# Last tile of a two-layer Fourier and expert kernel: scores read from PSUM, whole blocks exchanged over two queues, put-off rows added by accumulating transfers

## The chip, the cores and the metric

The kernel runs on one core of one Trainium2 chip. The metric is the device time of one execution in microseconds (us), the median of several runs. The engines of a core work from instruction queues of their own, in order, and wait for each other through semaphores: TensorE (PE in the profile, its weight loads PEld) multiplies matrices into PSUM, VectorE (DVE) and ScalarE (ACT) work on the on-chip memories SBUF and PSUM, GpSimd (POOL) on SBUF, and SyncE (SP) issues most transfers. The transfers of all queues run on 16 DMA engines.

## The reference

Two layers work on x, 2048 tokens of 512 numbers. Each layer adds a Fourier mixing of the normalised rows, and then a sum over experts picked by product keys:

```python
x = x + _A_ref(_layernorm(x), dft_seq_re, dft_seq_im, dft_hid_re, dft_hid_im)
x = x + _B_ref(_layernorm(x), w_q, k1, k2, u, v)      # and both once more

# _A_ref: the real part of a two-dimensional Fourier transform, by matrices
y = einsum("ts,bse->bte", seq_re, x @ hid_re.T) - einsum("ts,bse->bte", seq_im, x @ hid_im.T)

# _B_ref: 32 heads, 2 x 16 keys each, 2 x 2 best, of these the 2 best of 256 experts
s1, s2 = q1 @ k1.T, q2 @ k2.T                          # per token and head, 16 scores each
t1, i1 = the two largest of s1;  t2, i2 = the two largest of s2
cand = t1[:, None] + t2[None, :];  eidx = i1[:, None] * 16 + i2[None, :]
g, e = softmax of the two largest of cand, their eidx
out = sum over heads and picks of g * gelu(x . u[e]) * v[e]
```

## The kernel before

**Tiles.** The 2048 tokens are 16 tiles of 128 (`P`). The sequence transform of a layer is done in units: seven of two tiles (256 tokens) and two of one tile (tiles 14 and 15). In layer 1 the units run in the order 0, 7, 1 to 6, 8, so tiles 12 and 13 (unit 6) come last but one and tile 15 (unit 8) last. `seq_unit` multiplies the normalised rows (`xh`, `xl`, high and low parts) with the sequence matrices (`ch`, `cl`) into `acc` (L519); `token_tile` does the rest for one tile.

**One tile** (`token_tile`). TensorE multiplies the transform with the hidden matrices (L659), VectorE adds it to the row (L669), statistics are taken (L255 to L264, one step on GpSimd, L261), the row is scaled (L272, L697), transposed (L747 or through memory) and cast in two parts (L752, L757). TensorE makes 2 x 512 scores into two PSUM banks `pc` (L777, L781), ScalarE copies them to `sc` in SBUF, reordered (L786). VectorE picks the best two of 16 keys for each of 64 half-heads: a tree of maxima (L867, L876, the helper `tree32`), a comparison with the maximum (`eq`, L861), its number (L903, L885), the removal of that entry (L912, L916), and the same again. From the picks (`q`) TensorE turns codes (L989), ScalarE copies them (`qt`, L993), VectorE makes one-hot masks (L1012, L1018), TensorE multiplies these in blocks of four tokens (L1028), and ScalarE copies the blocks to SBUF (L1038): a block is 4 x 4 small matrices of which the diagonal is wanted. That diagonal goes out to memory in four transfers and comes back, one token per partition, in two (`gdr`, `gt`; L1058, L1066). VectorE multiplies it with the activation (L1069), TensorE transposes it (L1100) and multiplies it with the expert values `vh`, `vl` in six steps (L1119, L1123). VectorE adds the product to the row (L1134), and SyncE stores the row (L1139).

**Put-off products.** For the 13 tiles of the first seven units of layer 1 that last product is put off (`DEFERRED`): the weights go to memory (`ptd`, L1091), the row to `xod`, and `off(z, ...)` does the rest in the last stretch, as soon as TensorE is done with the sequence transform: load the weights (L574), cast (L581), load the row (L585), six products into `acc` (L591), a copy by ScalarE (L597), a sum by VectorE (L600), a store (L601).

**Order.** Nothing is written out in its final order. Each step is an `Op` with its engine, a cost and a priority; `Plan.run` places them on the engines by these costs, and the program is emitted in that order. Each engine then runs its own list in order. Tile 15 has the priority `FINAL` and the flag `fine`: its first sum and scaling are done in halves, and its selection (`HALVED`) in two halves whose steps alternate. Where the plan sees a gap on TensorE after the last sequence product, it puts filler products in (L1205).

```python
a = op("PE", MM512, f, a0 + [a, seq_last], take=[hb] if n == 0 else [], prio=prio + (n,))
nc.scalar.copy(t["sc"][:, :, hf, :], t["pc", hf].rearrange("p h e -> p e h"))
nc.sync.dma_start(t["gdr"][:, :, k].rearrange("j e g f -> (j e) g f"), t["gs"][k::4, :, k, :])
```

## Time and profile before

| what | us |
|---|---|
| median of 3 runs | 1251.66 |
| lowest and highest | 1251.53, 1252.41 |
| the profiled execution, whole | 1250.42 |
| its span, first to last instruction | 1248.7 |
| TensorE busy | 1226.5 (98%) |
| VectorE busy | 1009.6 (81%) |
| ScalarE busy | 483.2 (39%) |
| granted TensorE clock | 1.000 |

The profile is of one execution; its times run from the start of the span. A busy time is the sum of an engine's instructions; neighbours on VectorE and TensorE overlap a little, so the distance from start to start is what a queue pays. A row of the order of time gives start, duration, engine, line and operation with `out<-in`, and how many were merged.

### The profile page before, as it was taken

The numbers are of one execution on the slowest core, as the hardware profiler recorded it, in microseconds if no ns is written. First come the engines' busy times: TensorE is split into PE (matmuls) and PEld (weight loads), VectorE is DVE, ScalarE is ACT, GpSimd is POOL, SyncE is SP. The second block draws the span as 40 slices with busy tenths as digits, with TensorE's granted clock in tenths as the row PEclk, the third lists the DMA queues.
The fourth block names the chain that finished last, engine by engine and source line by source line (L and its number), as shares of the span: only waits on it lengthen the run. The fifth ranks groups of instructions, "written<-read, shape, count | busy, mean of one in ns | idle before, by whom it ended". The sixth has DMA issues, their size and how long they took to land.

```text
span 1248.7 us, 20707 instructions
## 1 busy us (share of the span) xinstructions
PE 1226.5 (98%) x7576; PEld 1015.0 (81%) x7576; DVE 1009.6 (81%) x2290; ACT 483.2 (39%) x994; POOL 44.5 (4%) x71
## 2 busy tenths in 40 slices
PE   9999999999999999999999999999999999999997
PEld 6877778777887888899878888777888888888985
DVE  8899997988988876869877458969595877969797
ACT  7522244333333333433563233333333333333543
POOL 2000000000000000000000000000000000000000
PEclk9999999999999999999999999999999999999999
DMA  7866551343434244341556232443526343353554
GB/s 239 263 197 223 179 159 35 85 89 93 99 92 105 67 100 111 76 119 58 129 135 153 93 104 54 122 101 90 139 76 144 85 110 85 102 118 94 127 169 127
DMA packets 317766, 148.19 MB, mean 119 GB/s; under 512 B 221920, under 2 KB 287968, under 8 KB 317664
## 3 DMA queue, kind: packets, MB, share of 16 engines
q1 hardware_dynamic: 317664, 146.87, 44.3%
q8 instruction: 59, 0.97, 0.3%
q14 instruction: 43, 0.35, 0.1%
HBM read 120.86 MB, written 25.95 MB: 118 GB/s over the span
## 4 chain that ended last, share of the span: by engine, by line
PE 64%; DVE 20%; issue 6%; DMA 5%; ACT 2%; SPq 2%; POOL 1%; POOLq 0%; DVEq 0%; ACTq 0%
PE acc L519 36%; PE bank L659 9%; PE bank L777 6%; PE bank L781 3%; DVE cl L463 2%; PE bank L808 2%; DVE eq L861 2%; DVE w L385 1%; DMA raw<-x2d 1%; PE bank L519 1%; DVE lr L1012 1%; PE bank L393 1%; DVE tmp L867 1%; DVE eq L885 1%; DMA gdr<-sc 1%
## 5 line engine op out<-in xcount | busy, mean ns | idle before, releaser
L519 PE MATMUL acc<-ch,xh 128*128 128x512 f32 (+1 forms) x868 | 328.7, 379 | 1.7 <-DVE ptl L548 1.7
L519 PE MATMUL acc<-cl,xh 128*128 128x512 f32 (+1 forms) x868 | 321.9, 371 | 0.0
L519 PE MATMUL acc<-ch,xl 128*128 128x512 f32 (+1 forms) x868 | 321.8, 371 | 0.0
L459 ACT CAST ch<-raw 128x512 fp32r<-128x512 f32 x256 | 158.5, 620 | 277.5 <-PE acc L519 235.3
L463 DVE TENSOR_TENSOR cl<-raw,ch 128x512 fp32r<-128x512 f32 x256 | 175.1, 686 | 49.1 <-ACT ch L459 38.4
L519 PEld LDWEIGHTS acc<-ch,xh 128*128 128x128 f32 x868 | 163.7, 189 | 29.3 <-issue 1.8
L519 PEld LDWEIGHTS acc<-cl,xh 128*128 128x128 f32 x868 | 163.6, 188 | 28.8
L519 PEld LDWEIGHTS acc<-ch,xl 128*128 128x128 f32 x868 | 163.8, 189 | 25.2
L777 PE MATMUL bank<-wh,tok 128*128 128x512 f32 x256 | 100.3, 392 | 2.4 <-ACT tok L735 2.4
L659 PE MATMUL bank<-dh,pth 128*128 128x512 f32 (+1 forms) x264 | 102.4, 390 | 0.2
L659 PE MATMUL bank<-dl,pth 128*128 128x512 f32 (+1 forms) x264 | 100.6, 383 | 0.0
L777 PE MATMUL bank<-wl,tok 128*128 128x512 f32 x256 | 99.7, 390 | 0.0
L867 DVE TENSOR_TENSOR tmp<-sc 128x512 f32<-128x512 f32 (+1 forms) x66 | 44.3, 671 | 66.9 <-ACT sc L786 66.5
L1012 DVE TENSOR_TENSOR lr<-iota,qt 128x1024 f16<-128x1024 f16 x124 | 80.5, 683 | 21.6 <-ACT qt L993 21.6
L659 PE MATMUL bank<-dh,ptl 128*128 128x512 f32 (+1 forms) x264 | 95.6, 384 | 0.0
L786 ACT COPY sc<-bank 128x512 f32<-128x512 f32 x64 | 37.1, 587 | 127.8 <-PE bank L781 83.3
L261 POOL TENSOR_TENSOR stats<-stats,half 128x1 f32<-128x1 f32 x64 | 43.2, 681 | 1160.7 <-DVE stats L258 1081.3
L861 DVE TENSOR_TENSOR eq<-sc,val 128x1024 f16<-128x1024 f32 (+1 forms) x66 | 78.6, 1190 | 1.6
L519 PE MATMUL acc<-ch,xg 128*128 128x512 f32 (+1 forms) x204 | 77.1, 378 | 0.0
L519 PE MATMUL acc<-cl,xg 128*128 128x512 f32 (+1 forms) x204 | 75.8, 372 | 0.1
L519 PE MATMUL acc<-ch,xm 128*128 128x512 f32 (+1 forms) x204 | 75.6, 371 | 0.0
L781 PE MATMUL bank<-wh,tok 128*128 128x512 f32 x256 | 68.6, 390 | 1.1 <-DVE tok L738 1.1
(166 smaller groups left out, 2045.2 us busy)
## 6 DMA issues: line engine op xcount, KB each, us to landing
raw<-in_cseq SPq DMA_DIRECT2D x224, 256.0 KB, 2.9
wr<-in_wq SPq DMA_DIRECT2D x32, 512.0 KB, 3.9
raw<-in_ctile SPq DMA_DIRECT2D x32, 256.0 KB, 2.9
xdr<-lr SPq DMA_DIRECT2D x25, 256.0 KB, 2.3
tok<-xdr SPq DMA_DIRECT2D x100, 64.0 KB, 2.6
wr<-in_x SPq DMA_DIRECT2D x16, 256.0 KB, 3.6
row<-in_x SPq DMA_DIRECT2D x16, 256.0 KB, 3.4
x2d<-row SPq DMA_DIRECT2D x16, 256.0 KB, 2.2
```

The source lines that it names most:

```text
L261: nc.gpsimd.tensor_tensor(st[:, 1:2], st[:, 1:2], half, op=ALU.pow)
L459: nc.scalar.copy(t[1], t[0])
L463: nc.vector.tensor_sub(t[2], t[0], as32(t[1]))
L519: nc.tensor.matmul(target(d), w[s][:, d * P:(d + 1) * P], moving(s % per, part), start=(s == 0 and k == 0 and d % blocks == 0), stop=(s == ...
L659: nc.tensor.matmul(t["y", cs.start], w[:, k, c, t0:t0 + P], r[:, c, k, cs], start=(z == 0 and c == 0 and m == 0), stop=(z == len(steps) - ...
L777: nc.tensor.matmul(t["pc", hf], t["th"][:, k, :], r[:, k, hf], start=(k == 0 and r is wh), stop=False)
L781: nc.tensor.matmul(t["pc", hf], t["tl"][:, k, :], wh[:, k, hf], start=False, stop=(k == KD - 1))
L786: nc.scalar.copy(t["sc"][:, :, hf, :], t["pc", hf].rearrange("p h e -> p e h"))
L808: nc.tensor.matmul(t["xu"], w[:, k, :], r[:, k, :], start=(m == 0), stop=(m == 3 * KD - 1))
L861: nc.vector.tensor_tensor(t["eq"][:, :, cols], flat("sc")[:, :, cols], val(rank_, cols), op=ALU.is_equal)
L867: nc.vector.tensor_max(t["tmp"][:, :, cols], flat("sc")[:, :8, cols], flat("sc")[:, 8:, cols])
L1012: nc.vector.tensor_tensor(t["m", hf, r], io2, row_of(r, hf), op=ALU.is_equal)
```

## The change

Three things are changed, all of them in the last stretch.

*Put-off rows.* The row of a put-off tile is stored in `out` itself and not in `xod`. ScalarE copies the product from PSUM into the buffer that held the weights, and GpSimd issues one transfer that adds it to the row in memory (`accum_op`). The load of the row, the sum on VectorE and SyncE's store are gone.

*Selection of tile 15.* The scores are not copied. Each half works on its PSUM bank as soon as it is there: the maximum is one `tensor_reduce`, the comparison reads PSUM, and the removal reads PSUM and writes `sc`; the second maximum is a reduction over `sc`. The other tiles keep the tree and the copy.

*Exchange and end of tile 15.* The blocks go out whole, in two halves of 256 KB, one issued by SyncE and one by ScalarE, and the diagonal is taken by the address steps of the two reads, again one from each queue. The product with the expert values is done in two halves of 256 columns in banks of their own, and each half is added and stored by itself, one from SyncE and one from ScalarE.

```diff
-        a1 = op("SP", load(256), lambda: nc.sync.dma_start(t["row"], xod[i]), a0 + [kept], prio=prio, lag=2.3)
...
-        a = op("ACT", act(512), f_ev, [a], take=[hv], last=[hb], prio=prio)
-        a = op("DVE", dve(512), lambda: nc.vector.tensor_add(t["row"], t["row"], t["ev"]), [a, a1], last=[hv], prio=prio)
-        op("SP", load(256), lambda: nc.sync.dma_start(out[i * P:(i + 1) * P, :], t["row"]), [a], prio=prio, lag=2.3)
+        a = op("ACT", act(512), lambda: nc.scalar.copy(t["row"], t["po"]), [a], last=[hb], prio=prio)
+        op("POOL", 1.0, lambda: nc.gpsimd.dma_start(out[i * P:(i + 1) * P, :], t["row"], accum_op=ALU.add), [a, kept], prio=prio, lag=3.0)
...
-            kept = op("SP", load(256), lambda: nc.sync.dma_start(xod[i], t["row"]), [b], last=[hrow], prio=prio, lag=2.3)
+            kept = op("SP", load(256), lambda: nc.sync.dma_start(out[i * P:(i + 1) * P, :], t["row"]), [b], last=[hrow], prio=prio, lag=2.3)
...
+        def largest(rank_, cols, w, scores, after, prio, **kw):
+
+            def f():
+                new()
+                nc.vector.tensor_reduce(t["val"][:, rank_, cols], scores(), axis=AX.X, op=ALU.max)
+            return [op("DVE", dve(16 * w), f, after, prio=prio, **kw)]
...
+                nc.vector.scalar_tensor_tensor(flat("sc")[:, :, cols], t["eq"][:, :, cols], -BIG, scores(), op0=ALU.mult, op1=ALU.add)
...
+        if fine:
+            left, a_val, a_key, first = [], [], [], []
+            for f in range(2):
+                part = slice(f, f + 1), slice(f * H, (f + 1) * H), 32
+                order_ = prio + (f,)
+                a = largest(0, *part[1:], lambda f=f: t["pc", f], scored[f:f + 1], order_, **hold, behind=first)
+                first = first + a
+
+                def view(f=f):
+                    return t["pc", f].rearrange("p h e -> p e h")
+
+                a = eq(0, *part[1:], view, a, order_)
+                a = code(0, *part, a, order_)
+                left += without(*part, view, a, order_, last=banks[f:f + 1], take=[] if f else [hsc])
...
+                a = largest(1, *part[1:], lambda c=part[1]: flat("sc")[:, :, c].rearrange("p e c -> p c e"), left[f:], order_)
...
+        if fine:
+            queue = (("SP", nc.sync), ("ACT", nc.scalar))
+            for hf in range(2):
...
+                    d = bass.AP(d.tensor, d.offset + hf * 8 * STEP, [[ROW, P], [STEP, 8], [1, 4 * E]])
+                    queue[hf][1].dma_start(d, t["gs"][:, 8 * hf:8 * hf + 8].rearrange("p g t e -> p g (t e)"))
...
+                    d = bass.AP(d.tensor, d.offset, [[STEP, 64], [4 * ROW, E], [1, E]])
+                    queue[j][1].dma_start(t["gt"][j * 64:(j + 1) * 64], d)
...
+                a_ph = op("PE", 4 * MM256, f_high, [a_ph], take=[hbs[c]], prio=prio)
...
+                a_ph = op("PE", 2 * MM256, f_lower, [a, a_ph], last=[hpp], prio=prio)
+                b = op("DVE", dve(256), lambda c=c, cs=cs: nc.vector.tensor_add(t["row"][:, cs], t["row"][:, cs], t["po", c]),
+                       [a_ph], last=[hbs[c]], prio=prio)
+                q = (("SP", nc.sync), ("ACT", nc.scalar))[c]
+                op(q[0], 0.4, lambda q=q, cs=cs: q[1].dma_start(out[i * P:(i + 1) * P, cs], t["row"][:, cs]), [b], last=[hrow],
+                   prio=prio, lag=2.6)
```

Since the plan places everything anew, the order moves with it. In the rows that follow, `x2` behind a row means that many of it in a row.

VectorE around the start of tile 15's selection, before. `lr` are the masks of tile 13, `xl<-xl,xg` the sums of put-off rows, `tmp<-sc` the first maximum of tile 15:

```order
L1012 TENSOR_TENSOR lr<-iota,qt 128x1024 x2
L697 TENSOR_SCALAR tok<-row,stats 128x256
L1018 TENSOR_TENSOR lr<-lr,qt 128x1024
L1012 TENSOR_TENSOR lr<-iota,qt 128x1024
L757 TENSOR_TENSOR tok<-bank,tok 128x256 x2
L1018 TENSOR_TENSOR lr<-lr,qt 128x1024
L1069 TENSOR_TENSOR act<-act,gt 128x256
L600 TENSOR_TENSOR xl<-xl,xg 128x512 x3
L867 TENSOR_TENSOR tmp<-sc 128x8x32
```

The same place after. `val<-bank` is the first maximum of tile 15:

```order
L688 TENSOR_SCALAR tok<-row,stats 128x256
L1025 TENSOR_TENSOR lr<-iota,qt 128x1024
L748 TENSOR_TENSOR tok<-bank,tok 128x256 x2
L1025 TENSOR_TENSOR lr<-iota,qt 128x1024 x2
L1031 TENSOR_TENSOR lr<-lr,qt 128x1024
L1025 TENSOR_TENSOR lr<-iota,qt 128x1024
L858 TENSOR_REDUCE val<-bank 128x32
L851 TENSOR_TENSOR eq<-bank,val 128x16x32
```

The scaling of tile 15 moved ahead of tile 13's masks; the sums, tile 12's product (`act<-act,gt`) and the last multiplication of tile 13's masks (`lr<-lr,qt`) left the place, the latter two to behind the selection.

SyncE at the end of the program, before. `gdr<-sc` is the exchange of tile 13, `gdr<-pth` and `raw<-gdr` that of tile 15, `out<-xl` are put-off rows:

```order
L1058 DMA gdr<-sc 32x16x16 x4
L601 DMA out<-xl 128x512
L1066 DMA gt<-gdr 64x16x16 x2
L1058 DMA gdr<-pth 32x16x16 x4
L601 DMA out<-xl 128x512 x3
L1066 DMA raw<-gdr 64x16x16 x2
L1139 DMA out<-row 128x512
L601 DMA out<-xl 128x512
L1139 DMA out<-row 128x512
L601 DMA out<-xl 128x512 x4
L1139 DMA out<-row 128x512
L601 DMA out<-xl 128x512
```

SyncE at the end of the program, after. `gds<-pth` is one half of tile 15's blocks, `raw<-gds` one of its two reads, the 256-column store its first half of columns:

```order
L1090 DMA gdr<-sc 32x16x16 x4
L1077 DMA gds<-pth 128x8x64
L1097 DMA gt<-gdr 64x16x16 x2
L1083 DMA raw<-gds 64x16x16
L1189 DMA out<-row 128x512
L1178 DMA out<-row 128x256
L1189 DMA out<-row 128x512
```

No put-off row is issued here any more; the other halves of tile 15's transfers stand on ScalarE, and tile 13's whole row is the last store where tile 15's stood one place from the end.

TensorE's last products, before. `acc<-vh,xh` are put-off products, `acc<-dh` filler, `bank<-vh,pp` the product of a tile that is not put off:

```order
L591 MATMUL acc<-vh,xh 128x512
L591 MATMUL acc<-vl,xh 128x512
L591 MATMUL acc<-vh,xh 128x512 x2
L1205 MATMUL acc<-dh 128x512 x11
L1100 MATMUL bank<-identf,act 128x128 x2
L1119 MATMUL bank<-vh,pp 128x512
L1119 MATMUL bank<-vl,pp 128x512
```

TensorE's last products, after. `bank<-vh,ch` are the products of tile 15, `bank<-vh,pp` those of tile 13:

```order
L1255 MATMUL acc<-dh 128x512 x9
L1131 MATMUL bank<-identf,act 128x128 x4
L1167 MATMUL bank<-vh,ch 128x256
L1167 MATMUL bank<-vl,ch 128x256
...
L1172 MATMUL bank<-vh,ch 128x256 x4
L1150 MATMUL bank<-vh,pp 128x512
L1150 MATMUL bank<-vl,pp 128x512
```

Tile 13's transposes moved next to those of tile 15, and its products behind tile 15's. GpSimd's list before ends with the 64 steps of the statistics; now 13 transfers (`out<-xl`) follow them.

## Rows read from the trace of the kernel before

**Rows 1.** Stretches: start:end, length, busy of PE, PEld, DVE, ACT, POOL, clock, DMA, GB/s.
```profile
1215.00:1220.00 5.00, 5.00 (x55) 4.11 (x54) 5.00 (x21) 2.59 (x7) 0.00 (x0) 1.00 0.02 3
...
1240.00:1245.00 5.00, 3.40 (x15) 2.26 (x13) 1.81 (x4) 0.37 (x1) 0.00 (x0) 1.00 0.84 319
```

**Rows 2.** The chain that ended last: start, duration, what.
```profile
1241.52 0.23 PE bank L1100 x2
...
1243.89 0.69 DVE row L1134
```

**Rows 3.** TensorE in order of time: start, duration, line, operation, count.
```profile
1197.48 0.40 PE L591 MATMUL acc<-vh,xh 128*128 128x512 f32 x1
...
1202.26 1.12 PE L659 MATMUL bank<-dh,ptl 128*128 128x256 f32 x8
...
1208.38 0.39 PE L777 MATMUL bank<-wh,tok 128*128 128x512 f32 x1
...
1216.21 0.50 PE L591 MATMUL acc<-vl,xh 128*128 128x512 f32 x1
...
1223.85 1.29 PE L1205 MATMUL acc<-dh 128*128 128x512 f32 x5
```

**Rows 4.** VectorE in order of time, 1205 to 1241 us.
```profile
1205.89 0.16 DVE L264 SCALAR_TENSOR_TENSOR stats<-stats 128x1 f32<-128x1 f32 x1 [0.44 <-POOL stats L261]
1205.97 1.29 DVE L1012 TENSOR_TENSOR lr<-iota,qt 128x1024 f16<-128x1024 f16 x2
...
1210.30 1.89 DVE L600 TENSOR_TENSOR xl<-xl,xg 128x512 f32<-128x512 f32 x3
1212.11 0.41 DVE L867 TENSOR_TENSOR tmp<-sc 128x256 f32<-128x256 f32 x1
...
1225.56 0.21 DVE L956 TENSOR_TENSOR q<-key,df 128x128 f16<-128x128 f16 x1
...
1226.96 0.68 DVE L1012 TENSOR_TENSOR ch<-iota,raw 128x1024 f16<-128x1024 f16 x1
...
1240.28 0.42 DVE L1069 TENSOR_TENSOR act<-act,raw 128x256 f32<-128x256 f32 x1
```

**Rows 5.** The stretch of the selection, VectorE's line L867 alone.
```profile
1211.00:1226.00 15.00, 1.67 (x4) 1.00 0.16 55
```

**Rows 6.** The same stretch, VectorE's line L876 alone.
```profile
1211.00:1226.00 15.00, 2.81 (x12) 1.00 0.16 55
```

**Rows 7.** VectorE's groups by shape: count, busy us, mean ns, idle before.
```profile
L398 DVE TENSOR_REDUCE ws<-bank 128x128 f32<-128x384 f32 x32 | 17.9, 560 | 0.0
```

**Rows 8.** ScalarE's groups by shape, 1203 to 1245 us.
```profile
L752 ACT CAST tok<-bank 128x256 fp32r<-128x256 f32 x2 | 0.8, 376 | 0.3 <-PE bank L747 0.3
L272 ACT ACTIVATE tok<-row,stats 128x256 f32<-128x256 f32 x1 | 0.6, 602 | 0.0
```

**Rows 9.** SyncE's issues in order of time, 1225 to 1249 us.
```profile
1231.93 2.63 SPq L1058 DMA_DIRECT2D gdr<-pth  x4
...
1236.36 1.38 SPq L1066 DMA_DIRECT2D raw<-gdr  x2
...
1244.98 0.43 SPq L601 DMA_DIRECT2D out<-xl  x1
```

**Rows 10.** Transfers issued in 1200 to 1249 us: KB each, median us to landing.
```profile
out<-xl SPq DMA_DIRECT2D x13, 256.0 KB, 2.6
xl<-xod SPq DMA_DIRECT2D x3, 256.0 KB, 2.9
...
gdr<-pth SPq DMA_DIRECT2D x4, 32.0 KB, 2.1
raw<-gdr SPq DMA_DIRECT2D x2, 64.0 KB, 2.9
```

**Rows 11.** Instructions on `out`: issue ns, shortest, median, longest.
```profile
L601 SPq DMA_DIRECT2D out<-xl x13: 332/433/806, 1211.0 to 1245.0; - x13
```

**Rows 12.** GpSimd in order of time, 1200 to 1249 us.
```profile
1204.93 0.92 POOL L261 TENSOR_TENSOR stats<-stats,half 128x1 f32<-128x1 f32 x1 [44.26 <-DVE stats L258]
```

More of the change, by code (lines that the diff above doesn't have):

```diff
@@ L839, in flat @@
             return t[name].rearrange("p e f h -> p e (f h)")
-        halved = HALVED(layer, at)
-        cuts = [(slice(f, f + 1), slice(f * H, (f + 1) * H), 32) for f in range(2)] if halved else [(slice(0, 2), slice(0, 64), 64)]
+        both = (slice(0, 2), slice(0, 64), 64)
         def val(rank_, cols, m=16):
@@ L910, in f_one, with without @@
+        def without(fs, cols, w, scores, after, prio, **kw):
+            nf = fs.stop - fs.start
             def f_one():
@@ L924, in chain @@
-            heq.users += 1
-            return a_val, a_key
-        begun = []
-        a_val, a_key = [], []
-        for z, (fs, cols, w) in enumerate(cuts):
-            x, y = chain(z, fs, cols, w, [sc_parts[z]] if halved else sc_parts, prio + (z,) if halved else prio)
-            a_val += x
-            a_key += y
+                if fine and fs.start == 0:
+                    t["sc"] = work([P, E, 2, H], F32, "sc")
+                nc.vector.scalar_tensor_tensor(flat("sc")[:, :, cols], t["eq"][:, :, cols], -BIG, scores(), op0=ALU.mult, op1=ALU.add)
@@ L935, in v @@
+        for o in a_key:
+            o.last.append(heq)
+            heq.users += 1
         def v(rank_, hf):
@@ L1102, in f_ph @@
         def f_ph():
[L1103 removed]
+            t["pp"] = apool.tile([P, 2, T], F32R, name="ch", bufs=BUFS["c"]) if fine else work([P, 2, N], F32R, "pp")
             t["ph"], t["pl"] = (t["pp"][:, m].rearrange("p (k t) -> p k t", t=P) for m in range(2))
@@ L1138, in token_tile @@
                     o.behind.extend(back)
-            stores.append(op("SP", load(256), lambda: nc.sync.dma_start(out[i * P:(i + 1) * P, :], t["row"]), [a],
+            stores.append(op("SP", 0.45, lambda: nc.sync.dma_start(out[i * P:(i + 1) * P, :], t["row"]), [a],
                              last=[hrow], prio=prio, lag=2.3))
```

182 lines of the change are left out of this document (101 added, 81 removed).

## The prediction, made before the changed kernel ran

> **What bounds the kernel now.** I read the stretches first, then the chain of work that ended last, then the engines' order of time around the last tile (token tile 15, the only one with the FINAL priority). Nearly all of the span is the matmul-bound middle, and the instruction order of that part is the same in both programs; they part only from about 1185 us on. So the whole question is the last 65 us. In [rows 1] the reader is to see that VectorE, not TensorE, is full from 1215 to 1220 with the transfers idle, and that from 1240 to 1245 it is the other way round: VectorE 1.81 of 5 us, transfers at 0.84. [rows 2] shows what closes the run: tile 15's transposes at 1241.52, then its row's sum at 1243.89. Followed back through [rows 4, 9], tile 15's path is: scores at 1208.38 [rows 3], selection on VectorE from 1212.11 to 1225.77 (13.66 us), masks from 1226.96, gate blocks out from 1231.93 in four issues, back from 1236.36, product at 1240.28, last sum 1243.89, end of span 1248.7. I put the new program on this clock, stage by stage.
>
> **Up to the scores.** Four put-off products stand inside tile 15's first sum, from 1197.48 on [rows 3]; now all 78 stand behind it. One costs 0.2315: the 33 of them from 1216.21 to 1223.85 took 7.64 [rows 3]. So that sum ends not at 1203.38 but 4 x 0.23 = 0.93 sooner, and the last step of the statistics falls from 1205.89 to 1204.96 [rows 4]. From there to the first score matmul it was 2.49. In it the scaling of the second half waited for two of tile 13's masks (1.29, [rows 4]) and two products stood ahead on TensorE (0.46). Now one mask stands behind the scaling and one product ahead of the scores. What must remain is the scaling (0.60), one cast (0.38) [rows 8], four transposes and the handoffs, together about 1.75 by estimate (bounds 1.0 and 2.49). Scores start at 1206.7, 1.7 sooner.
>
> **Selection.** Before, the scores were copied by ScalarE, and three sums of put-off rows (1.89) held VectorE until 1212.11 [rows 4]. Both are gone from here. VectorE now has, after the statistics, the scaling, one mask that waits for tile 13's turned codes (about 1206.9), two small differences and four 0.6 us operations on tile 13's masks: it is free at 1210.05. The first score bank is done at 1206.7 + 12 x 0.2315 + 0.1 = 1209.6, so VectorE sets the start: 1210.05, 2.1 sooner. One multiplication of tile 13 now stands behind the selection (0.6).
> Each of the four searches for a maximum was four operations, 1.67 + 2.81 = 4.48 us busy in all [rows 5, 6], 1.12 each; it becomes one reduction over 512 elements. The nearest row, a reduction of 384 elements out of PSUM at a 64-byte step, takes 0.56 [rows 7], so 0.75 for 512. Busy time saved is 4 x 0.37 = 1.5; since neighbours overlap, the time saved lies between 0.7 and 1.5, and I take 1.1. Reading PSUM instead of SBUF I cost at nothing, by that same row. The selection ends at 1210.05 + 13.66 - 1.1 = 1222.6. TensorE meanwhile does the scores (24 wide matmuls and 12 half ones, 6.95) and then 40 put-off products, 9.26: it comes to the transposes of the codes at 1222.9. The products are thus late by 0.3, and 1222.9 counts: 2.9 sooner than 1225.77.
>
> **Masks and blocks.** From the codes to the first mask it was 1.40, part of it three other VectorE operations; now the copy through ScalarE decides and I take 1.0: 1223.9. VectorE has in between the multiplication and a product of tile 12 (0.95), covered by that wait. From the first mask to the first issue it was 4.97 [rows 4, 9]; the same six masks, matmuls and copy remain: 1228.85.
>
> **The exchange through memory.** Four issues took 2.63 and two reads 1.38, on SyncE alone [rows 9]. The reads could not start until the fourth had landed: 1231.93 to the product at 1240.28 is 8.35. Now each half goes out in one issue, the second from ScalarE at 1228.85. The first is ready sooner, but SyncE has tile 13's four issues ahead (about 1226.0 to 1228.6), so both go at nearly the same time. Landing: 2.1 for a 32 KB piece, 2.9 for a 256 KB load, 2.6 for a 256 KB store [rows 10]. Each half is a 256 KB store, in 256-byte pieces; I take 2.6 and keep 2.1 and 4.5 (2.9 plus 512 KB at the 319 GB/s of [rows 1]) as ends. Both landed at 1231.4. The reads leave SyncE behind tile 13's two (1.38, about 1231.5) and ScalarE behind a copy of a put-off product (about 1231.9), and take 2.9 [rows 10]: product at 1234.9, 5.4 sooner. This stage gains 2.3.
> By the row, then, four issues in series (2.63) outlast the landing of one piece (2.1), and splitting them over two queues is worth its price. The Trainium skill, "DMA: Bandwidth & Descriptors", section "Issuing engines are not separate DMA queues", says that issuing from several engines saves only the issue time, and calls that usually small beside the transfer. Small it is not here; were nothing of it saved, the time would be about 1249.2.
>
> **The end.** From the product to the last sum it was 3.61 [rows 2, 4]. In it the transposes waited about 0.8 for filler matmuls; the filler now ends near 1235.0 and covers nothing. But tile 13's row now comes last, behind tile 15's twelve half-wide matmuls (12 x 0.116 = 1.39) and a second cast (0.38): 3.61 - 0.8 + 1.39 + 0.38 = 4.6, last sum at 1239.5. From there to the end it was 4.81, and one store followed the last row's (1244.98, [rows 9]); without it 4.45. Span 1243.95, 4.75 less. The profiled execution took 1250.42 with a span of 1248.7; the median of the runs is 1251.66, so these stand 1.24 above the profiled one. Forecast: 1251.66 - 4.75 = 1246.9.
>
> **The put-off rows.** Thirteen loads of stored rows, thirteen sums on VectorE (0.6 each, 7.8 in all) and thirteen stores by SyncE go; thirteen accumulating transfers of GpSimd come, each behind ScalarE's copy. The loads and ten of the sums lay beside other work, so their removal is counted only where named above. The first copy is done at about 1204.5, the last at about 1233.3 (78 products, less what stands before). No row has a GpSimd transfer. Issue: 0.33 to 0.81 on SyncE, and GpSimd's own operation 0.92 beside a busy VectorE [rows 11, 12]; I take 1.0. Landing: a store's 2.6 at least, a load and a store, 5.5, at most [rows 10]. The last lands at 1233.3 + 1.0 + 5.5 = 1239.8, while the path's last store goes out at about 1240: off the path, at nothing, as long as GpSimd keeps up with one per 2.4 us.
>
> **Rivals.**
> *GpSimd sets the end (slower).* If it cannot issue while VectorE works, and VectorE is 5.00 of 5 us busy [rows 1], all thirteen start when VectorE first rests, about 1229. At p each, the end is 1229 + 13p + 5.5 + 1.7 (landing to end of span): p = 1.0 gives 1249.2, no change; from p = 1.15 the kernel is slower by over 0.2%; p = 1.5 gives a span of 1255.7, a time of 1258.7. Against it: GpSimd's one operation at 1204.93 ran beside a busy VectorE and was done in 0.92 [rows 12]. The Trainium skill, "SBUF — State Buffer", section "Who interferes with whom", has such a lock, though only for VectorE instructions in a two-port mode, which it denies to tensor_tensor, nearly all that runs here; no run shown here can tell.
> *The new reads are slow (no change).* If the eight operations that read scores in PSUM or at a step (four reductions, two comparisons, two removals) take twice their 0.65, the selection is 5.2 longer, less 0.3 of slack: 1251.8. Against it, [rows 7].
> *Bytes, not issues, price the exchange.* 512 KB go out where 128 KB did. At the 4.5 end, 1.9 more: 1248.8.
> *More than worked out.* Without tile 13's issues ahead on SyncE, and with the selection's end free of products, up to 2.5 more: 1244.4.
>
> **How the numbers follow.** The forecast as worked, its terms at their ends giving 1244.6 to 1249.1, gets 0.55; more gain 0.10; slow reads 0.10; the bytes 0.10, half of it still over 0.2% (2.5 us, about what a measurement can tell from no change) faster; GpSimd 0.15, of which 0.12 slower. Faster: 0.55 + 0.10 + 0.05 = 0.70; same: 0.10 + 0.05 + 0.03 = 0.18; slower 0.12. The range 1244.0 to 1251.5 leaves out the slow GpSimd and part of the larger gain.
>
> **What would show it.** Selection starting near 1210 and ending 12 to 12.6 later; eight new reads at 0.56 to 0.75; the first mask near 1224; two issues at about 1228.7 and a product near 1235; tile 13's sum the last; GpSimd's thirteen issues spread from 1204 to 1235 at about 1 us each. It would be wrong if these issues bunch up behind 1229, if the halves land after more than 4.5, or if ScalarE, which now also issues, comes late to a copy.

## The result: slower by 0.3%

| what | before | after |
|---|---|---|
| median, us (11 runs of each, side by side) | 1250.3 | 1254.6 |
| ratio of the two, with 95% interval | | 1.0031 [1.0022, 1.0039] |
| span of the profiled execution, us | 1248.7 | 1253.7 |

The forecast was 1246.9, faster, in a range up to 1251.5. The changed kernel takes 1254.6: 4.3 us more by the two medians, 3.9 us (0.31% of 1250.3) by the ratio, which is the figure used from here on. The first half of the stage-by-stage forecast, up to the first mask, held; the second did not.

VectorE of the changed kernel in order of time (start, duration, line, operation, shapes, idle time before and what ended it); the rows answer to [rows 4]. `val<-bank` is the first maximum, `q<-key,df` the last step of the selection, `ch<-iota,raw` the first mask of tile 15, `act<-act,gt` the product of tile 13's exchanged blocks, `act<-act,raw` that of tile 15's, the last row tile 13's sum:

```profile
1210.16 0.68 DVE L858 TENSOR_REDUCE val<-bank 128x32 f32<-128x512 f32 x1
...
1216.02 1.06 DVE L858 TENSOR_REDUCE val<-sc 128x32 f32<-128x512 f32 x1
...
1223.83 0.22 DVE L969 TENSOR_TENSOR q<-key,df 128x128 f16<-128x128 f16 x1
...
1225.00 0.69 DVE L1025 TENSOR_TENSOR ch<-iota,raw 128x1024 f16<-128x1024 f16 x1
...
1241.20 0.42 DVE L1100 TENSOR_TENSOR act<-act,gt 128x256 f32<-128x256 f32 x1 [9.22 <-DMA gt<-gdr]
1243.23 0.42 DVE L1100 TENSOR_TENSOR act<-act,raw 128x256 f32<-128x256 f32 x1 [1.61 <-DMA raw<-gds]
...
1249.79 0.69 DVE L1184 TENSOR_TENSOR row<-row,bank 128x512 f32<-128x512 f32 x1 [1.54 <-PE bank L1154]
```

Up to the first mask the rows stand within 1.1 us of the forecast (selection from 1210.05, mask at 1223.9). Then VectorE is idle for 9.22 us, and what ends the idle time is not tile 15's read but tile 13's. The forecast counted tile 13's issues on SyncE, but gave its transfers no landing and its product no place on VectorE. Tile 15's product, 1234.9 in the forecast, is at 1243.23; the last sum, 1239.5, at 1249.79.

What filled the gap stands in the stretches of the changed kernel (busy of PE, PEld, DVE, ACT, POOL, granted clock, DMA share, GB/s), to be read against [rows 1]:

```profile
1215.00:1220.00 5.00, 5.00 (x24) 4.14 (x23) 4.95 (x14) 2.28 (x4) 2.62 (x3) 1.00 0.51 63
1220.00:1225.00 5.00, 4.19 (x26) 2.94 (x26) 4.82 (x23) 2.48 (x9) 2.36 (x3) 1.00 1.06 154
...
1230.00:1235.00 5.00, 5.00 (x23) 4.13 (x23) 1.02 (x2) 2.01 (x4) 1.74 (x2) 1.00 1.33 186
1235.00:1240.00 5.00, 1.13 (x5) 0.59 (x4) 0.00 (x0) 0.58 (x1) 0.87 (x1) 0.87 1.20 149
1240.00:1245.00 5.00, 1.48 (x5) 0.71 (x5) 1.34 (x4) 0.74 (x2) 0.00 (x0) 0.50 0.61 117
```

The DMA share is 1 or more from 1220 to 1240, and yet only 149 to 186 GB/s move; before, a share of 0.84 moved 319, and in this place the share was 0.02 and 0.00 from 1215 to 1225, 0.38 and 0.45 from 1225 to 1235, and 0.90 from 1235 to 1240. So transfers that move few bytes for the time they take fill the place where the exchange runs. And TensorE, with 1.13 of 5 us busy from 1235 to 1240, has a granted clock of 0.50 (1.2 of 2.4 GHz) from 1240 to 1245.

The transfers issued from 1199 us on, of the changed kernel (first row: a queue, its packets, MB and share of the 16 engines' time; others: KB each, median us from issue to landing), answer to [rows 10]:

```profile
q0 software_dynamic: 1872, 3.41, 43.2%
...
out<-xl POOLq DMA_DIRECT2D x13, 256.0 KB, 4.9
...
gdr<-sc SPq DMA_DIRECT2D x8, 32.0 KB, 4.1
gt<-gdr SPq DMA_DIRECT2D x4, 64.0 KB, 4.8
gds<-pth ACTq DMA_DIRECT2D x1, 256.0 KB, 5.0
gds<-pth SPq DMA_DIRECT2D x1, 256.0 KB, 5.8
...
raw<-gds ACTq DMA_DIRECT2D x1, 64.0 KB, 5.0
raw<-gds SPq DMA_DIRECT2D x1, 64.0 KB, 6.1
```

q0 is GpSimd's queue. The packets of its 13 accumulating transfers take 43.2% of the time of all 16 engines through 54.7 us: 23.6 us, or 1.82 us each. This is packet time, here and below. It is no proof that the engines can do nothing else meanwhile, since shares over 1, such as the 1.33 above, show that packets overlap in this count. The exchange's transfers beside them land in 4 to 6 us instead of 2 to 3. GpSimd itself was not the limit. Of its 13 issues in the changed kernel these are the first, one in the middle of the stretch in which VectorE is 4.95 of 5 us busy, and the last; all 13 waited for ScalarE's copy:

```profile
1205.58 1.04 POOL L592 DMA_DIRECT2D out<-xl  x1 [0.32 <-ACT xl L591]
...
1219.06 0.87 POOL L592 DMA_DIRECT2D out<-xl  x1 [0.47 <-ACT xl L591]
...
1238.03 0.87 POOL L592 DMA_DIRECT2D out<-xl  x1 [3.39 <-ACT xl L591]
```

SyncE's queue and one row of ScalarE's in the changed kernel show the same from the issuing side, against [rows 9]:

```profile
1226.90 3.53 SPq L1090 DMA_DIRECT2D gdr<-sc  x4
1230.48 1.21 SPq L1077 DMA_DIRECT2D gds<-pth  x1
1235.30 1.61 SPq L1097 DMA_DIRECT2D gt<-gdr  x2
1237.00 2.86 SPq L1083 DMA_DIRECT2D raw<-gds  x1
```
```profile
1237.04 0.58 ACT L591 COPY xl<-acc 128x512 f32<-128x512 f32 x1 [3.69 <-DMA gds<-pth]
```

The single issue of a read takes 2.86 us, where two took 1.38 before. And a copy of a put-off product stands on ScalarE behind the read that waits for the halves (3.69): the last accumulating transfer goes out so late for that reason. With the halves at 5.0 and 5.8 and a copy that ScalarE comes late to, two of the forecast's three signs of being wrong are there.

### The profile page after: what moved, and what is told of

It reads as the page before. It is cut to its first block, busy times and chain, and to the rows that moved or that the text cites. A ratio compares the mean times of both kernels' runs of the same rounds, so it can differ in the third digit from the quotient of the medians.

```text
span 1253.7 us, 20656 instructions
## 1 busy us (share of the span) xinstructions
PE 1227.0 (98%) x7571; PEld 1015.2 (81%) x7571; DVE 1002.2 (80%) x2266; ACT 482.7 (38%) x992; POOL 55.7 (4%) x84
## 3 DMA queue, kind: packets, MB, share of 16 engines
q0 software_dynamic: 1872, 3.41, 1.9%
## 4 chain that ended last, share of the span: by engine, by line
PE 69%; DVE 19%; DMA 5%; issue 2%; ACT 2%; SPq 2%; POOL 1%; DVEq 0%; ACTq 0%
PE acc L517 38%; PE bank L650 11%; PE bank L768 7%; PE bank L772 4%; DVE cl L461 3%; PE bank L802 2%; DVE eq L851 2%; DMA gdr<-sc 2%; DVE lr L1025 1%; DVE w L383 1%; PE bank L517 1%; PE bank L391 1%; DVE eq L887 1%; DMA raw<-x2d 1%; DVE eq L881 1%
## 5 line engine op out<-in xcount | busy, mean ns | idle before, releaser
L864 DVE TENSOR_TENSOR tmp<-sc 128x512 f32<-128x512 f32 x62 | 42.6, 687 | 66.9 <-ACT sc L777 66.5
```

The costliest lines, as they stand in the source:

```text
L864: nc.vector.tensor_max(t["tmp"][:, :, cols], flat("sc")[:, :8, cols], flat("sc")[:, 8:, cols])
```

## The experiments

Where tile 15's last sum into its row falls (`row<-bank,row`, 1203.54 before) lies between 1202.2 and 1206.9, also where the instruction order up to it is the same (after 1203.27, e1 1206.34). It goes with the set of runs that was timed side by side: where the kernel before took 1250.3 to 1250.7 (after; e5 to e8; e13 to e15) the sum stands at 1202.2 to 1203.5, where it took 1252.6 to 1253.1 (e1 to e4; e9 to e12; e16, e17) at 1204.0 to 1206.9. Why is open. So profiles are compared by distances behind that sum, and times by ratios to the kernel before on the same chip. Stages in us: to the start of the selection, to its last step (`q<-key,df`), to tile 15's product (`act<-act,raw`), to the last sum of any row, to the end of the span.

| kernel | start | selection | product | last sum | end | time, ratio to before |
|---|---|---|---|---|---|---|
| before | 8.57 | 13.45 | 14.72 | 3.61 | 4.81 | 1 |
| after | 6.89 | 13.67 | 19.40 | 6.56 | 3.91 | 1.0031 [1.0022, 1.0039] |
| e1, after with plain stores | 6.90 | 13.68 | 14.17 | 5.89 | 3.92 | 0.9983 [0.9973, 0.9993] |
| e2, after with old put-off rows | 7.96 | 13.37 | 15.01 | 4.77 | 4.07 | 0.9998 [0.9989, 1.0007] |
| e3, before with accumulating alone | 7.52 | 13.45 | 18.21 | 4.92 | 3.86 | 1.0026 [1.0016, 1.0036] |
| e4, after with the old exchange | 6.89 | 13.68 | 19.88 | 5.52 | 3.65 | 1.0018 [1.0009, 1.0027] |
| e5, after, more filler | 6.90 | 13.67 | 19.39 | 4.51 | 3.96 | 1.0015 [1.0006, 1.0024] |
| e15, e1 with more filler | 6.89 | 13.69 | 14.06 | 4.51 | 3.96 | 0.9972 [0.9962, 0.9983] |
| e6, before, old issues on two queues | 8.57 | 13.44 | 14.72 | 3.83 | 3.77 | 0.9994 [0.9985, 1.0003] |
| e7, before with whole blocks alone | 8.56 | 13.44 | 14.18 | 3.12 | 5.00 | 0.9988 [0.9979, 0.9997] |
| e9, before with the selection alone | 7.96 | 13.37 | 17.67 | 3.08 | 4.96 | 1.0011 [1.0002, 1.0019] |
| e13, e9 with more filler | 7.96 | 13.37 | 16.12 | 3.06 | 5.02 | 1.0004 [0.9995, 1.0013] |
| e8, before, 5 rows added | 8.41 | 13.49 | 14.73 | 3.09 | 3.95 | 0.9986 [0.9977, 0.9995] |
| e12, e8 with whole blocks | 8.41 | 13.49 | 14.54 | 4.10 | 3.94 | 0.9995 [0.9985, 1.0004] |
| e14, e12 with more filler | 8.41 | 13.50 | 14.20 | 3.07 | 3.96 | 0.9987 [0.9978, 0.9996] |
| e10, 5 rows added, old end | 7.78 | 12.94 | 14.04 | 3.07 | 4.04 | 0.9983 [0.9972, 0.9993] |
| e11, e10, new end, filler | 7.79 | 12.95 | 15.58 | 2.89 | 3.72 | 0.9984 [0.9975, 0.9992] |
| e16, e10 with 8 rows added | 6.89 | 13.29 | 15.49 | 5.77 | 3.93 | 0.9995 [0.9985, 1.0005] |
| e17, e10 with 11 rows added | 6.89 | 13.31 | 18.48 | 5.76 | 3.72 | 1.0015 [1.0006, 1.0024] |

### Is it the accumulating? (e1, e3, e4)

The theory: an accumulating transfer holds the transfer engines, and the exchange queues behind it. Rivals: the 512 KB of whole blocks are themselves too much, or GpSimd's way of issuing. e1, which is to part them, leaves the row itself out of the sum for 13 tiles.

```diff
e1, in the changed kernel:
-  nc.gpsimd.dma_start(out[i * P:(i + 1) * P, :], t["row"], accum_op=ALU.add)
+  nc.gpsimd.dma_start(out[i * P:(i + 1) * P, :], t["row"])
e3, in the kernel before: off(...) and the store of the row as in the changed kernel, nothing else
e4, in the changed kernel, tile 15's exchange as before:
-  if fine:
-      queue = (("SP", nc.sync), ("ACT", nc.scalar))
+  if False:
+      queue = (("SP", nc.sync), ("ACT", nc.scalar))
```

> The changed kernel with one difference: GpSimd's thirteen transfers store the put-off product instead of adding it to the row in memory (so 13 of the 16 tiles of the output hold the product alone). Same instructions, same order, same bytes out of SBUF. Theory A (the adding keeps the 16 DMA engines busy, and the exchange of tiles 13 and 15 queues behind it): the transfers' share of the DMA engines falls from 1.83 us of all 16 to about 0.7 each, the two halves of tile 15's blocks land in under 3.5 us instead of 5.0 and 5.8, its reads in under 3.5 instead of 5.0 and 6.1, TensorE's clock stays at full speed to the end, and the time is 1246 to 1248. Rival B (the whole blocks in 256-byte pieces and the stepped reads are slow in themselves): landings stay at 5 to 6, time 1253 to 1255. Rival C (it is GpSimd's way of issuing, whatever the transfer does): as B.

> The kernel before with one part of the change alone: the put-off rows added by GpSimd's accumulating transfers. Selection, exchange in four issues and end of tile 15 as before. Theory A: the four small transfers of each exchange land in 4 to 6 us instead of 2.1 and the reads in 5 instead of 2.9, so the time is slower than before, 1253 to 1258 where before is 1250.3. Rival B: no slower than before, 1247 to 1250.5, since the sums on VectorE and 26 transfers of SyncE are gone.

> The changed kernel with tile 15's exchange as before the change: the diagonal in four issues of 32 KB and two reads, all from SyncE, in place of two halves of 256 KB from two queues. Theory A: small pieces queue behind the accumulating transfers just the same, landings 4 to 6 us, and the issues in series come on top: 1254 to 1258, no better than the 1254.6 of the changed kernel. Rival B: landings back at 2.1 to 3 us, 1249 to 1252.

With the same bytes from the same queue at the same places, but not accumulated, tile 15's product stands 14.17 instead of 19.40 behind the selection (e1). With accumulating alone in the kernel before, it stands 18.21 behind it instead of 14.72, and the kernel is slower by 0.26% (e3), as the theory had it. With the old exchange of 128 KB it is 19.88 (e4): the loss does not come from the blocks' bytes. e4's time, 1252.5, lies between its two expectations, and is less than that of the changed kernel (1.0018 against 1.0031). e1 fell short of its expectation in three things: the time, 0.9983, is just above the expected one, the halves landed in 3.7 and 3.9 and not under 3.5, and the clock fell all the same.

### The clock (e5, e15)

In the changed kernel TensorE's last rows show the second loss. Idle for 5.64 us, then its products at the granted clock of 0.50 (rows of the changed kernel's TensorE, 1241 to 1250 us):

```profile
1241.77 0.66 PE L1131 MATMUL bank<-identf,act 128*128 128x128 f32 x2 [5.64 <-DVE act L1100]
...
1244.87 0.58 PE L1167 MATMUL bank<-vh,ch 128*128 128x256 f32 x1 [0.46 <-ACT ch L1136]
```

e1 falls to 0.50 from 1244 to 1246 us too. So the changed kernel and e1 got more filler, and nothing else:

```diff
+  extra = {tile 13's transposes: 24, tile 15's transposes: 4, its first product: 1}     # e5; in e15 1, 4, 1
   for o in order:
       if o.engine == "PE":
+          for _ in range(extra.get(o, 0)):
+              fill(1)
```

> The changed kernel with more filler products on TensorE near the end: 24 more of 128x512 ahead of tile 13's transposes, 4 ahead of tile 15's, one ahead of the last product. Nothing else differs. If the granted clock of 0.50 behind TensorE's idle stretch is a cost of its own, the last products (4.4 us at half clock from 1244.87) take about 2.2, the last sum stands 4.5 instead of 6.6 behind tile 15's product with the activation, and the time is about 2 us below the changed kernel's, 1.0015 of the kernel before instead of 1.0031. If only the transfers decide, the clock is full and the time is unchanged (1.003).

> The changed kernel with plain stores in place of the accumulating ones (the stored row is left out of the sum) and six more filler products near the end, so that the clock is full in it as in the changed kernel with filler. The difference to that one is then the accumulating alone. If accumulating costs transfer time only, that is the 5.2 us by which tile 15's product stands later with it (19.4 against 14.2 behind the codes), 0.4%: 0.9970 to 0.9980 here against 1.0015. If half the loss was the clock, 0.9990.

Stretch of e5, the same 5 us in which the changed kernel had 0.50, and the selection's last step, the product and the last sum of VectorE in e5 and then in e15:

```profile
1240.00:1245.00 5.00, 3.95 (x23) 2.69 (x22) 1.61 (x4) 0.75 (x2) 0.00 (x0) 1.00 0.46 98
```
```profile
1223.04 0.23 DVE L969 TENSOR_TENSOR q<-key,df 128x128 f16<-128x128 f16 x1
...
1242.43 0.42 DVE L1100 TENSOR_TENSOR act<-act,raw 128x256 f32<-128x256 f32 x1 [1.81 <-DMA raw<-gds]
...
1246.94 0.69 DVE L1184 TENSOR_TENSOR row<-row,bank 128x512 f32<-128x512 f32 x1 [0.88 <-PE bank L1154]
```
```profile
1224.07 0.23 DVE L969 TENSOR_TENSOR q<-key,df 128x128 f16<-128x128 f16 x1
...
1238.13 0.43 DVE L1100 TENSOR_TENSOR act<-act,raw 128x256 f32<-128x256 f32 x1 [1.58 <-DMA raw<-gds]
...
1242.64 0.69 DVE L1184 TENSOR_TENSOR row<-row,bank 128x512 f32<-128x512 f32 x1 [0.88 <-PE bank L1154]
```

From product to last sum both take 4.51, where the changed kernel took 6.56: the clock is worth 2.05 us in the profile, and the time of e5 is 1.0015 where the changed kernel's is 1.0031 (2.0 us), as expected. e5 and e15 differ in nothing but the accumulating (and in 29 and 6 fillers, in TensorE's idle time): 19.39 against 14.06 us to the product, 5.33 us; in the times 1.0015 against 0.9972, 0.43% or 5.4 us, also as expected. Profile and time are two measurements that agree. That is the price of the thirteen accumulating transfers, and it comes without a share of the clock. GpSimd's issues are longer too when they accumulate (0.86 to 1.04 us against 0.54 to 0.72 in e15), but GpSimd is idle between them in both.

The transfers of e15, issued from 1199 us on, beside those of the changed kernel above:

```profile
q0 software_dynamic: 1040, 3.41, 16.3%
...
out<-xl POOLq DMA_DIRECT2D x13, 256.0 KB, 2.3
...
gds<-pth SPq DMA_DIRECT2D x1, 256.0 KB, 3.7
gds<-pth ACTq DMA_DIRECT2D x1, 256.0 KB, 3.9
...
raw<-gds SPq DMA_DIRECT2D x1, 64.0 KB, 3.5
raw<-gds ACTq DMA_DIRECT2D x1, 64.0 KB, 3.8
```

The same 3.41 MB, 16.3% of 47.6 us: 0.60 us of all engines for one transfer instead of 1.82. The Trainium skill, "DMA: Bandwidth & Descriptors", section "SDMA does more than copy", describes the addition as done in line with the stream; here the packets of a transfer that adds take three times as long.

### The exchange without accumulating (e2, e6, e7)

```diff
e2, in the changed kernel: off(...), xod and the store of the row as before
e6, in the kernel before, tile 15 alone: issue k and read j go to (nc.sync, nc.scalar)[k % 2], [j]
e7, in the kernel before: the exchange of tile 15 (two halves, two reads, two queues) as changed
```

> The changed kernel with the put-off rows as before the change (rows in memory of their own, loaded, summed by VectorE, stored by SyncE); selection, exchange and end of tile 15 stay changed. Theory A: exchange lands in 2.2 to 3.5 us, time below before by 1 to 3 us (some of the thirteen sums stand before the selection again), 1247.5 to 1249.5 where before is 1250.3. Rival B: landings of 5 to 6 us remain, time 1252 or more.

> The kernel before, in which alone tile 15's four diagonal issues and two reads alternate between SyncE and ScalarE (for all bytes as before, 128 KB out). If the issues in series price the exchange, as the prediction had it, 2.63 becomes about 1.3 and 1.38 about 0.7: codes to product 14.7 becomes 12.8, and the time falls by 1.9 us (0.9985). If landing and ScalarE's own work decide, codes to product stays at 14 to 14.7 and the time within 0.1%.

> The kernel before, in which alone tile 15's blocks go out whole in two halves on two queues and the diagonal is taken by the reads; put-off rows, selection and end as before. By the prediction's terms (a half lands in 2.6, a read in 2.9) the time falls by about 2.3 us (0.998). If 512 KB in pieces of 256 bytes are priced by their bytes and pieces (halves 3.4 to 4.4, reads 3.0 to 4.0), codes to product stays at 14.2 to 15.2 and the time within 0.1%; slower by over 0.1% if the halves land later than 4.5 beside the stores of put-off rows.

Transfers of e7 from 1224 us on:

```profile
gds<-pth SPq DMA_DIRECT2D x1, 256.0 KB, 2.9
gds<-pth ACTq DMA_DIRECT2D x1, 256.0 KB, 3.6
...
raw<-gds SPq DMA_DIRECT2D x1, 64.0 KB, 3.0
raw<-gds ACTq DMA_DIRECT2D x1, 64.0 KB, 4.1
```

Whole blocks alone bring tile 15's product 0.54 us nearer (14.18 against 14.72), not 2.3. The later half lands in 3.6 and the later read in 4.1, where 2.6 and 2.9 were taken. The time, 0.9988, lies between the two expectations. Spreading the old issues over two queues (e6) moves the product not at all; VectorE of e6:

```profile
1238.79 0.69 DVE L600 TENSOR_TENSOR xl<-xl,xg 128x512 f32<-128x512 f32 x1 [0.84 <-ACT xg L597]
1239.40 0.42 DVE L1070 TENSOR_TENSOR act<-act,raw 128x256 f32<-128x256 f32 x1
```

There is no idle time ahead of the product: it waits its turn behind a put-off sum, which waits for ScalarE. Little was there to be won in any case: the later read landed 0.36 us sooner behind the selection (14.19 against 14.55), not 1.9. The rule that the prediction weighed and set aside (the Trainium skill, "DMA: Bandwidth & Descriptors", section "Issuing engines are not separate DMA queues": several issuing engines save only issue time, usually small) is nearer to this: even the issue time saved was not seen at the product. The whole new last tile with the old put-off rows (e2), from which a gain of 1 to 3 us was expected, is no faster than the kernel before (0.9998); its halves landed in 3.4 and 4.4.

### The selection (e9, e13)

```diff
e9, in the changed kernel: put-off rows, exchange and end as before, so that the selection alone is changed
e13: e9, with filler products: 4 ahead of the codes, 2 ahead of and 2 behind the second blocks, 1 and 1 at the end
```

> The kernel before, in which alone tile 15's selection is the changed one (scores read from PSUM, four reductions in place of the trees); put-off rows, exchange and end as before. By the prediction's terms (0.75 for each reduction, no copy of the scores) the selection is 1.1 us shorter and the time at least that much less, 0.999. By the rows of the changed kernel (1.06 for each reduction over scores in SBUF, 13.7 to 13.9 in all) the selection is as long as before and the time within 0.05% (0.9995 to 1.0005).

> The kernel with the changed selection alone, and ten more filler products on TensorE around tile 15's codes, masks and last transposes. If the 0.11% that the changed selection cost alone is the granted clock of 0.50 from 1235 to 1238 in that run, and not the selection, the clock stays full and the time comes to the kernel before, 0.9990 to 1.0003. If the selection itself costs it (longer reductions, VectorE's queue), 1.001 as without the filler.

The selection itself is as long as before (13.37 against 13.45), as the second expectation had it, though the time, 1.0011, lies above both: two reductions take 0.68 from PSUM, but the two over `sc` take 1.06. The loss of e9 comes later, and by the two profiles half of it is the clock again. Stretches of e9, and of e13 at the same stage:

```profile
1234.00:1236.00 2.00, 1.41 (x4) 1.03 (x4) 2.00 (x5) 1.76 (x3) 0.00 (x0) 0.73 0.52 53
1236.00:1238.00 2.00, 2.00 (x6) 1.59 (x5) 1.40 (x3) 0.45 (x1) 0.00 (x0) 0.50 0.58 135
```
```profile
1230.00:1232.00 2.00, 1.87 (x9) 1.20 (x8) 2.00 (x5) 1.62 (x3) 0.00 (x0) 1.00 0.51 52
1232.00:1234.00 2.00, 2.00 (x11) 1.64 (x10) 2.00 (x5) 0.73 (x2) 0.00 (x0) 1.00 0.54 100
```

With full clock the product stands 16.12 behind the selection instead of 17.67, 1.55 of the 2.95 us lost there. The times, 1.0011 and 1.0004, have intervals that overlap and can't show this by themselves. The rest to 14.72, 1.4 us, is order: in e13 too the product follows a put-off sum without idle time. The start that the selection gained (0.61) is less than what these later sums take back. e13's interval, 0.9995 to 1.0013, allows no difference and excludes the 1.1 us gain (0.9991).

### How many rows may be added? (e8, e12, e14, e10, e11, e16, e17)

```diff
+  ADDED = 5                                              # e16: 8, e17: 11
-  for z, parts in enumerate(put_off):  off(z, *parts)
+  for z, parts in enumerate(put_off):  (off_add if z < ADDED else off)(z, *parts)
e8: this alone, in the kernel before; off_add is the changed kernel's off, off the old one
e12: e8 with whole blocks as in e7; e14: e12 with 8 and 1 fillers ahead of the last transposes and product
e10: ADDED = 5 in the changed kernel, second maximum by tree32, the end in one bank as before
e11: e10 with the changed end and 13 fillers
```

> The kernel before, in which alone the first five of the thirteen put-off rows are added by accumulating transfers of GpSimd; the other eight, the selection, the exchange and the end are as before. If an accumulating transfer harms only the transfers that run beside it (about 1.8 us of all 16 engines each), these five are done before tile 15's exchange, its landings stay at 2.1 to 2.9, VectorE comes to the selection 1 to 2 us sooner, and the time is 0.5 to 1.5 us less (0.999). If accumulating harms in another way (GpSimd, ScalarE's copies, the stores of rows), the time is that of all thirteen, 1.001 to 1.003.

> The kernel before with two parts: five of the thirteen put-off rows added by GpSimd's transfers, and tile 15's blocks whole on two queues; selection and end as before. If the gains add, 0.9974; if the exchange's gain is hidden behind the same VectorE sums and stores that the five rows took away, 0.9985 as with the five rows alone.

> The kernel with five put-off rows added by GpSimd and whole blocks on two queues, and nine more filler products ahead of tile 15's last transposes and product. If the two gains failed to add because TensorE, idle for 2.1 us there, fell to the clock of 0.50 behind it (products twice as long: 1.2 us more), the time falls to 0.9975 to 0.9985. If they hide each other, it stays at 0.9990 to 1.0000.

> Five of the thirteen put-off rows added by GpSimd's transfers, eight as before; tile 15's scores from PSUM, its second maximum by the tree again; whole blocks on two queues; the end in one bank as before. If accumulating harms only what runs beside it, the gains of the parts add: 1.6 us for the five rows, 1.3 for the exchange, and up to 1.4 for the selection's start, where VectorE with five rows added waits 1.56 for ScalarE's copy of the scores: 0.9965 to 0.9975. If one part's gain is hidden behind another's (VectorE's sums, the stores of the other eight rows on SyncE), it stays at 0.998 to 0.999.

> As the kernel with five rows added and all else changed, but with the changed end too (product in two halves of 256 columns, two stores) and 13 more filler products that keep TensorE's clock up. If the end in halves saves anything at full clock, it is 0.3 to 0.6 us below that kernel (0.05%); if the twelve narrow products ahead of tile 13's cost what the prediction gave them (1.39 and a cast of 0.38), it is 0.5 to 1.5 us above it.

> As the kernel with five rows added and scores from PSUM, second maximum by the tree, whole blocks on two queues and the old end, but with the first eight put-off rows added by GpSimd's transfers; the eighth is issued some 3 us ahead of tile 15's exchange. If accumulating harms only what runs beside it, tile 13's exchange lands later (3 to 5 instead of 2.1) but tile 15's product keeps its 14.0 behind the codes, VectorE and SyncE lose three sums, three loads and three stores more, and the time is that of five rows or 0.1 to 0.5 us less: 0.9978 to 0.9985. If the harm grows with the number of rows added, it is 0.999 to 1.001.

> The same with eleven rows added; three of their transfers are issued while tile 13's and tile 15's blocks go out. If accumulating harms what runs beside it, halves and reads of tile 15 land in 4 to 6 instead of 2.9 to 4.0, its product stands 16 to 19 behind the codes, and the time is 2 to 4 us above that of five or eight rows: 1.000 to 1.002. If only the number of transfers at the very end counts, it stays at 0.998 to 0.999.

Five rows, added before the exchange begins, make the kernel before faster (e8, 0.9986, as expected), and tile 15's landings stay as they were. But the gain is not where it was expected, at the selection. It is behind the product: 3.09 instead of 3.61 to the last sum, and 3.95 instead of 4.81 from there, since no put-off store follows the last row. Ahead of the selection only 0.16 of the expected 1 to 2 us is won, as VectorE then waits for ScalarE's copy of the scores (e8):

```profile
1211.54 0.42 DVE L899 TENSOR_TENSOR tmp<-sc 128x256 f32<-128x256 f32 x1 [1.56 <-ACT sc L818]
```

With scores from PSUM and whole blocks (e10) the profile is 3.3 us shorter from that sum to the end (41.87 against 45.16), the time 0.9983, which is the expectation of gains that hide each other. With eight and eleven rows the medians rise to 0.9995 and 1.0015; five and eleven are clear of each other, five and eight are not. In e17 the halves go out while the last accumulating transfers run, and the reads when these are over (transfers of e17 from 1224 us on):

```profile
gds<-pth ACTq DMA_DIRECT2D x1, 256.0 KB, 7.0
gds<-pth SPq DMA_DIRECT2D x1, 256.0 KB, 7.5
...
raw<-gds SPq DMA_DIRECT2D x1, 64.0 KB, 3.1
raw<-gds ACTq DMA_DIRECT2D x1, 64.0 KB, 4.2
```

Halves 7.0 and 7.5, reads 3.1 and 4.2 as in e7: of tile 15's transfers those beside accumulating ones land late, and those behind them do not. Product (18.48) and time came as expected for e17.

Eight rows bring no more than five, against the expectation of 14.0 to the product: it stands at 15.49. The eighth, issued at 1228.24, takes 5.75 to land, only 0.6 us past the issue of SyncE's half at 1233.36, and the halves land in 3.8 and 4.1, little later than in e7. What else stands in the way is SyncE's queue, which is held up beside the eighth: tile 13's four pieces, issued from 1229.99, land in a mean 3.5 instead of 2.1, so tile 13's reads go out at 1235.41, and behind them and a put-off store tile 15's second read, 0.86 us after ScalarE's (SyncE's queue of e16):

```profile
1237.45 1.03 SPq L630 DMA_DIRECT2D out<-xl  x1
1238.58 0.57 SPq L1122 DMA_DIRECT2D raw<-gds  x1
```

The granted clock falls to 0.56 behind the longer wait. How much of the 1.45 us over e10's product (14.04) each of these costs, no run separates.

e12, at 0.9995 above both of its expectations, looked as if the gains of e7 and e8 hide each other. e14, with filler in TensorE's 2.1 us gap, comes to 0.9987, between its two. In the profiles the two gains then nearly add up: 0.86 us (e7) and 1.49 (e8) from the row's sum to the end, 2.02 together (e14). In the times they do not: 0.12% and 0.14%, together 0.13%. Which is right is open. In e11 the filler did harm: it delayed tile 13's transposes, ScalarE's cast behind them, and the read of tile 15 that ScalarE issues after the cast, which then landed in 4.8 instead of 4.0; its product stands 1.5 us later than e10's. Intervals of e7, e8, e10, e11 and e14 overlap: they are the versions that give the whole output and beat both kernels, 0.12 to 0.17% faster than before, and which is the best is not settled.

## Why the prediction was wrong, by its steps

The failed step is the one on **the put-off rows**: "off the path, at nothing, as long as GpSimd keeps up". It asked whether the issues and the last landing come in time. The issues did: 0.87 against 1.0, spread over 1205.6 to 1238.0. The landings, at a median of 4.9, lie within the bounds of 2.6 and 5.5, though the longest was 6.3. It did not ask what the transfers do to others on the 16 engines that all queues share. From [rows 10] it took a landing as the cost. The cost was 1.82 us of packet time of all 16 engines for each, where a plain store has 0.60, in the stretch in which the exchange of tiles 13 and 15 has to get through. Price: 5.4 us (e5 against e15).

**The clock** was no term at all; [rows 1] shows 1.00 in both stretches. The wait that the transfers made left TensorE without work, and the products behind it ran at the lower level, 0.50: 2.0 us (e5 against after).

**The exchange**: 12.3 from the end of the selection to the product were forecast, and even without accumulating and at full clock it is 13.8 (e15, 14.06 less the last step's 0.23). The landings are the mis-sized terms: 3.7 to 3.9 for 2.6, 3.5 to 3.8 for 2.9. Two halves in flight at once, in pieces of 256 bytes, were priced as one plain store. In e7, with SyncE's put-off stores beside them, the halves landed in 2.9 and 3.6 and the reads in 3.0 and 4.1. How much of this the second half, the small pieces and the stores beside them cost, no run separates. The rival "bytes, not issues" was the nearer one; it was charged with 1.9, and 1.5 came.

**The selection**: 12.6 forecast (1210.05 to 1222.6), 13.9 measured (1210.16 to 1224.05). The row of [rows 7] reads PSUM at a 64-byte step; it was used for four other reads. Tile 15's two reductions over PSUM read neighbouring elements and took 0.68, somewhat less than the 0.75 forecast; the two over `sc`, in SBUF at a 256-byte step, took 1.06. That is 0.62 of the 1.3 us; whether SBUF or the step makes it, no run separates. e10, with the tree there again, takes 12.94 to its last step, 0.73 less. The rest of the 1.3 is not resolved; 0.20 of it is a wait of VectorE for the second score bank, at 1212.81.

**The scores and the start** held: 2.1 us sooner were forecast, 0.93 of it in the row's sum itself and 1.2 behind it, where 1.68 came. The sum's own part can't be read from one profile, as its place moves by more than that. The times speak for it: in the eight kernels with the four products behind the sum (after, e1, e3, e4, e5, e15 to e17) the time stands a mean 1.2 us lower than the distances of the table say, from 2.2 lower to 0.5 higher; in the ten others the mean difference is nothing, from 0.6 lower to 1.2 higher. **The end** held too once the clock is full: 4.51 for 4.6, and 3.96 for 4.45.

The sum, with the times: e15, which is the change without accumulating at full clock, is 0.28% or 3.5 us below the kernel before, against 4.75 forecast: the exchange and selection cost 2.9 more than forecast, the end 0.6 less, which would leave 2.45, within the interval (2.1 to 4.8). From e15's 3.5 faster, 5.4 for accumulating and 2.0 for the clock lead to 3.9 slower. By times alone this comes out by construction, since each term is the difference of two neighbours in the row; what tests it is the profile, which gives 5.33 and 2.05 by itself. Of the rivals, GpSimd held up by VectorE is refuted (the issue at 1219.06 above, 0.87 while VectorE was 4.95 of 5 us busy, and issues that all waited for ScalarE); the slow-reads rival is right for two reductions and wrong in size. The slower outcome came by a mechanism that was not among them, so the 0.12 that the forecast gave to slower was for another reason.

What stays open: which of the faster versions is the fastest (their intervals overlap), why the gains of e7 and e8 add in the profiles and not in the times, and why tile 15's row sum stands up to 4.7 us apart between profiles, by the set of runs.

## To carry to other kernels

A transfer has two prices: its own landing, and the time its packets take on the transfer engines, which other transfers pay. Before calling one "off the path", look at what else is in flight in its place and add up the shares. When work is taken off an engine to shorten a wait, check that TensorE still has something to do in the new wait, or the products behind it may run at the lower clock, as they did here behind a wait of 5.64 us. A landing read from one transfer need not be that of another shape beside other traffic: 2.6 was read, and 2.9 to 3.9 came without accumulating.

## What the runs showed of the hardware

- The packets of an accumulating 256 KB transfer of GpSimd into rows in memory took 1.82 us of the time of all 16 engines (after), those of a plain one from the same queue 0.60 (e15); there were 144 against 80 of them (1872 and 1040 for 13). Median landing 4.9 against 2.3.
- Beside accumulating transfers a 32 KB piece landed in a median 4.1 (after) instead of 2.1 (before), a 256 KB half in 5.0 to 7.5 (after, e17) instead of 2.9 to 3.6 (e7) or 3.7 to 3.9 beside plain stores of GpSimd (e15), and one issue on SyncE took up to 2.86 us (after), where two took 1.38 before.
- GpSimd's issue took 0.86 to 1.04 us for an accumulating transfer (after), also where VectorE was 4.95 of 5 us busy, and 0.54 to 0.72 for a plain one (e15).
- A reduction of 512 elements took 0.68 us from PSUM with neighbouring elements and 1.06 from SBUF at a 256-byte step (after); one of 384 elements from PSUM at a 64-byte step 0.56 (before).
- The granted clock fell to 0.50 behind idle stretches of TensorE of 5.64 us (after) and 2.10 us (e12), and in e9 behind three shorter ones (1.36, 0.89 and 0.59 us from 1226 to 1235; 0.73 from 1234 to 1236, then 0.50). In e10 it stayed at 1.00 behind one of 1.74, so the length of a wait alone does not tell. With 29 and 9 products of filler in the wait it stayed at 1.00 (e5, e14).
